# Reordering four small pieces of the attention stage: two engines copy out a low-rank sum, a scaled copy moves behind the next q and k, a weight conversion moves behind the masks, one load moves behind another

## The chip, the cores and the metric

One core of one Trainium2 chip runs the whole kernel. The metric is device microseconds of one execution; the median of three runs of the kernel before is 671.45 us (670.75 to 672.5).

## The reference

A block-wise linear attention with a decay per head is followed by a channel mixer whose token mixing is a low-rank product. In short:

```python
# attention: B=4 batches, H=8 heads, S=768 positions, D=64
for each block of positions:
    intra = (q @ k.T * decay_mask) @ v
    inter = (q * lam**(pos+1)) @ kv_state
    out   = intra + inter
    kv_state = lam**block * kv_state + (k * lam**rev).T @ v
x = out, heads side by side          # (4, 768, 512)
# mixer: U (768, 32), V (32, 768), w_ch1 (512, 2048), w_ch2 (2048, 512), some of them in 8-byte floats
u   = x + (x.T @ U @ V).T
out = u + relu(u @ w_ch1) @ w_ch2
```

## The kernel before

**Tiles and steps.** The 4 x 768 positions are cut into 24 tiles of 128 positions, six to a batch. The attention stage is one loop over the tiles, s = 0 to 23, and c = s modulo 6 is the place in the batch. The order of every instruction in this stage is written out by hand: the list `pieces` (L629 to L657) holds names of small functions, and the loop at L761 calls them one after the other. Each engine runs its own share of that list strictly in this order, so a piece that stands earlier in the list can hold up everything behind it on the same engine.

**One step.** In step s the pieces do the following, in this order. `prep(s+1)` (L368) transposes the next tile's q and k on PE into the PSUM tile `pqk`, and ACT copies them out as `qt` and `kt` (L364). From the eighth step on, `turn` (L571) transposes a finished tile of u (L600) and `mix` (L544) adds the low-rank product (L551), both into `pm`. `scale` and `fade` let POOL and ACT multiply q, k and the state by the decay (L390, L379, L399). `split` and `mixed` are DVE's part of `turn` and `mix` (L620, L621, L563). `intra(s)` multiplies the masked scores `sm` with v into the PSUM tile `px` (L444), `state(s)` makes the next state in a PSUM tile that shares its place with `pqk` (L424), and `inter(s)` adds the old state's part to `px` (L455); then ACT copies `px` out as `x_nat` (L461). `turned` (L606 to L610) is the last part of `turn`: ACT writes the high part of u (L607) and POOL the difference (L608). `scores(s+1)` makes the next scores on PE (L406), and `masked(s+1)` multiplies them with the decay mask on DVE into `sm` (L415), for which the next step's `intra` waits. There is one buffer each for `px`, `pqk`, `pm` and the scores `pss`, so each is free again only when its reader is through.

**Batch ends.** In the last step of batches 0 to 2 (s = 5, 11, 17) `low` (L466) makes x^T U: 24 matmuls (48 in the records, two passes each) into 32-row groups of a PSUM tile `pp` that takes the place of `px`, and ACT copies the four groups to one row block `p_f` (L481). `low_rows` (L483) splits it: DVE makes the high part `p_h` (L511), and in the next step `next_of_low` lets ACT copy `p_h` to four places (L519), POOL make the low part (L523), and ACT copy that on (L530).

**Conversions beside it.** U, V and the weights come as 8-byte floats and are turned into floats by steps of their own, which `aside(s)` (L724) runs at given s. V's conversion is at s = 0, 3, 4 and 5. At s = 4 it has three DVE instructions (L186, L191, L689), and the same call issues a load of 128 KB of w_ch1's words. V's high part (four ACT copies, L696) is held back by `on_scalar_late` to step 5.

**Loads.** SP issues all loads but the first of k, in order. Before the loop it issues the first three tiles of q, k and v, with U's words (192 KB, `aside(-1)`) ahead of the third q. Later tiles are issued by `load_next` inside `prep` and `state`. There are three buffers for q and for v, and four for k.

**After the attention stage** come the first product of the mixer (L806, L816), into whose first units the last batch's low-rank work is threaded, and the second product (L939 to L943). Both are long rows of matmuls of 128x512.

Of the kernel before, what the change touches and what calls it, by code (L numbers as in the profile page):

```python
# [14 lines left out]
P = 128  # L15
# [3 lines left out]
def kernel(  # L19
# [28 lines left out]
    nc = tc.nc  # L48
# [3 lines left out]
    NT = S // P  # L52
# [4 lines left out]
    R = moe_U.shape[1]  # L57
    G = P // R
# [39 lines left out]
    def tmp(name):  # L98
        return wconv.tile([P, C], FP32, tag="tmp", bufs=3, name=name)
# [97 lines left out]
    def split_steps(tile_of, src, in_parts=False, scale=None, apart=False):  # L197
# [16 lines left out]
        def six():  # L214
            w, low = st["w"], st["o"][:, 1, :]
            st["low"] = low.bitcast(FP32) if scale is None else w
            nc.vector.tensor_tensor(
                out=low if scale is None else w, in0=w, in1=st["t"], op=ALU.subtract
            )
            if scale is not None:  # L220
                on_scalar(lambda: nc.scalar.mul(low, w, scale))
# [30 lines left out]
    def two_banks(name, tag):  # L252
        return psf.tile([P, 2, N], FP32, tag=tag, name=name)
# [7 lines left out]
    def bank(shape, name, tag):  # L261
        return psa[0].tile(shape, FP32, tag=tag, bufs=2, name=name)
# [8 lines left out]
    def load(name, s, engine):  # L271
        b, c = divmod(s, NT)
        t = raw_pool.tile(
            [P, H, D], FP32, tag=f"{name}raw", bufs=4 if name == "k" else 3, name=f"{name}raw"
        )
        source = {"q": q, "k": k, "v": v}[name]
        n = H if name == "v" else H // parts(s)
        for h in range(0, H, n):
            engine.dma_start(
                out=t[:, h : h + n, :],  # L280
                in_=source[b, h : h + n, c * P : (c + 1) * P, :].rearrange("h p d -> p h d"),
            )
        raw[s, name] = t
# [52 lines left out]
    kv = {}  # L336
# [124 lines left out]
        nc.scalar.copy(xs[s].rearrange("p (a x e) -> p x a e", a=HP, x=2), px)  # L461
        del st[s]

    pps = {}

    def low(b):  # L466

        pp = two_banks("pp", "px")[:, 0, 0:P] if b < B - 1 else bank([P, P], "pp", "b2")
        for c in range(NT):
            for g in range(G):  # L470
                nc.tensor.matmul(  # L471
                    out=pp[g * R : (g + 1) * R, :], lhsT=u_w[:, c, :],
                    rhs=xs[b * NT + c][:, g * P : (g + 1) * P],
                    start=(c == 0), stop=(c == NT - 1),
                )
        if b == B - 1:
            pps[b] = pp
            return
        pps[b] = rows_f = tmp("p_f")[0:R]
        for g in range(G):  # L480
            nc.scalar.copy(rows_f[:, g * P : (g + 1) * P], pp[g * R : (g + 1) * R])  # L481

    def low_rows(b):  # L483

        pp, t = pps.pop(b), tmp("p_h")[0:R]
        own = [(slice(g * R, (g + 1) * R), slice(g * P, (g + 1) * P)) for g in range(G)]
        if b == B - 1:
            h, h2, l, l2 = (p_hl[g * R : (g + 1) * R] for g in range(G))
            for rows, cols in own:
                nc.vector.tensor_scalar(  # L490
                    t[:, cols].bitcast(U32), pp[rows].bitcast(U32), HI, None, ALU.bitwise_and
                )

            def low_part():
                for rows, cols in own:
                    nc.vector.tensor_tensor(
                        out=l[:, cols], in0=pp[rows], in1=t[:, cols], op=ALU.subtract
                    )

            def spread():  # L500
                nc.scalar.copy(h, t)
                nc.scalar.copy(h2, t)

            def spread_low():
                nc.scalar.copy(l2, l.bitcast(FP32))

            pps[b] = [spread, low_part, spread_low]
            return

        rows_f = pp  # L510
        nc.vector.tensor_scalar(t.bitcast(U32), rows_f.bitcast(U32), HI, None, ALU.bitwise_and)  # L511
        wide = [slice(x * 2 * P, (x + 1) * 2 * P) for x in range(2)]

        def place(g, low):
            return p_hl[g * R : (g + 1) * R, wide[low]]

        def spread():
            for g in range(G):
                nc.scalar.copy(place(g, 0), t[:, wide[g // 2]])  # L519

        def low_part():
            for x in range(2):
                nc.gpsimd.tensor_tensor(  # L523
                    out=place(2 * x, 1), in0=rows_f[:, wide[x]], in1=t[:, wide[x]],
                    op=ALU.subtract,
                )

        def spread_low():
            for x in range(2):
                nc.scalar.copy(place(2 * x + 1, 1), place(2 * x, 1).bitcast(FP32))  # L530

        pps[b] = [spread, low_part, spread_low]
# [32 lines left out]
    uhl, ud, turned = {}, {}, {}  # L565
# [5 lines left out]
    def turn(s):  # L571

        g, n = divmod(s, TG)
        if n == 0:
            uhl[g] = hl_at[g >= FG].tile([P, 2, CT, N], F32R, tag="hl", name="u_hl")
            ud[g] = d_at[g >= FG].tile([P, CT, N], F32R, tag="d", name="u_d")
        cols = slice(n * P, (n + 1) * P)
        hi, low, diff = uhl[g][:, 0, :, cols], uhl[g][:, 1, :, cols], ud[g][:, :, cols]
        if g >= FG:
            pt = bank([P, CT, P], "put", "b1")  # L580
# [49 lines left out]
    for s in range(NS):  # L630
        b, c = divmod(s, NT)
        done = s - NT - 1
        more = s + 1 < NS
        turns = done > 0 and (done - 1) // TG < FG
        mixes = 0 <= done < NS - NT - 1
        rows = c == 0 and b > 0
        step = [("prep", s + 1)] * more
        step += [("turn", done - 1)] * turns + [("mix", done)] * mixes
        step += [("mix", done + 1)] * (not more)
        step += [("next_of_low", b - 1)] * rows + [("next_of_low", b - 1)] * rows  # L640
        step += [("scale", s + 1)] * more
        step += [("fade", s)] * (c > 0)
        step += [("late", s - 1)] * (1 < s < NT - 1 or s > NT)
        step += [("split", done - 1)] * turns
        step += [("mixed", done)] * mixes + [("mixed", done + 1)] * (not more)
        step += [("next_of_low", b - 1)] * rows
        step += [("intra", s), ("state", s), ("inter", s)]
        step += [("late", s)] * (s < 2 or s in (NT - 1, NT))
        step += [("turned", done - 1)] * (done > 0)
        step += [("scores", s + 1)] * more  # L650
        step += [("low", b)] * (more and c == NT - 1)
        step += [("aside", s)] * (0 < s < NT - 1 or s > NT)
        step += [("masked", s + 1)] * more
        step += [("low_rows", b)] * (more and c == NT - 1)
        step += [("aside", s)] * (s in (0, NT - 1, NT))
        step += [("store", done)] * (done >= 0 and done // TG < FG)
        pieces += step  # L657
    waiting = {name: list(range(NS)) for name in "qkv"}

    def load_next(name, engine=nc.sync):  # L660
        if waiting[name]:
            load(name, waiting[name].pop(0), engine)
# [3 lines left out]
        "prep": prep, "fade": fade, "scores": scores, "masked": masked, "inter": inter,  # L666
        "intra": intra, "state": state,
        "low": low, "low_rows": low_rows, "next_of_low": next_of_low, "mix": mix, "turn": turn,
        "mixed": mixed, "store": store, "split": lambda s: splits.pop(s)(),
        "scale": scale, "turned": lambda s: turned.pop(s)(),  # L670
# [53 lines left out]
    def aside(s):  # L724
        late.insert(0, None)
        for step in side.pop(s, ()):
            step()
        late.pop(0)
# [15 lines left out]
    load_next("k", nc.scalar)  # L744
    for name in "qkvkv":
        load_next(name)
    aside(-1)
    for name in "qkv":
        load_next(name)
    make_identity(nc, ident)  # L750
    pl = two_banks("pl", "pss")[:, 0, 0:H]
# [108 lines left out]
    c0, b = NS - NT, B - 1  # L860
# [131 lines left out]
    for i in range(len(steps) - STAG):  # L992
        g, ft = steps[i]
# [49 lines left out]
```

## Time and profile before

| What | Value |
|---|---|
| median of three runs | 671.45 us |
| the profiled execution | 669.36 us, of it 667.5 us span |
| PE busy | 656.7 us (98% of the span) |
| DVE / ACT / POOL busy | 490.1 / 281.5 / 115.1 us |
| chain that ended last | PE 94%, ACT 3%, DMA 2%, issue 1% |
| attention stage | 0 to about 117 us of the span |
| DMA share from 0 to 100 us | 0.84 to 1.03 in each stretch of 10 us |

The span is what the engines' records cover; the execution's own time lies 1.9 us above it. Times such as "at 64.6" are microseconds from the start of the span. In a row of the timeline the first two figures are start and length, and the bracket at the end is idle time of that engine just before the row with what ended it. In the chain of waits each piece is start, length and who held the chain.

### The profile page before, as it was taken

The numbers are of one execution on the slowest core, as the hardware profiler recorded it, in microseconds if no ns is written. First come the engines' busy times: TensorE is split into PE (matmuls) and PEld (weight loads), VectorE is DVE, ScalarE is ACT, GpSimd is POOL, SyncE is SP. The second block draws the span as 40 slices with busy tenths as digits, with TensorE's granted clock in tenths as the row PEclk, the third lists the DMA queues.
The fourth block names the chain that finished last, engine by engine and source line by source line (L and its number), as shares of the span: only waits on it lengthen the run. The fifth ranks groups of instructions, "written<-read, shape, count | busy, mean of one in ns | idle before, by whom it ended". The sixth has DMA issues, their size and how long they took to land.

```text
span 667.5 us, 13397 instructions
## 1 busy us (share of the span) xinstructions
PE 656.7 (98%) x5242; PEld 539.0 (81%) x5242; DVE 490.1 (73%) x856; ACT 281.5 (42%) x536; POOL 115.1 (17%) x98
## 2 busy tenths in 40 slices
PE   8899999999999999999999999999999999999997
PEld 7789889788888888888888888888888888888885
DVE  5669989878999777777796255886676775865864
ACT  4677886554555444444453122332322322322320
POOL 4456877330000000000000000030030300300300
PEclk9999999999999999999999999999999999999999
DMA  8999994354776655555578999753263352543531
GB/s 193 224 224 239 229 251 133 127 190 161 273 249 240 213 203 201 200 202 202 199 265 296 319 310 396 273 194 121 92 215 97 124 190 94 170 145 96 164 89 63
DMA packets 131776, 131.29 MB, mean 197 GB/s; under 512 B 81346, under 2 KB 89794, under 8 KB 131714
## 3 DMA queue, kind: packets, MB, share of 16 engines
q1 hardware_dynamic: 130512, 130.05, 61.3%
q8 instruction: 41, 0.67, 0.4%
q10 hardware_dynamic: 1202, 0.39, 0.2%
q14 instruction: 21, 0.17, 0.1%
HBM read 80.09 MB, written 50.33 MB: 195 GB/s over the span
## 4 chain that ended last, share of the span: by engine, by line
PE 94%; ACT 3%; DMA 2%; issue 1%; DVE 0%; ACTq 0%; DVEq 0%
PE pz L806 27%; PE pz L941 13%; PE pd L816 13%; PE pz L939 13%; PE pd L943 13%; PE pss L406 3%; PE px L444 3%; PE px L455 2%; PE pkv L424 1%; PE pqk L358 1%; DMA qraw<-in_q_dram 1%; DMA vraw<-in_v_dram 1%; PE pp L471 1%; DMA kraw<-in_k_dram 1%; PE pm L551 1%
## 5 line engine op out<-in xcount | busy, mean ns | idle before, releaser
L806 PE MATMUL pz<-u_hl,w 128*128 128x512 f32 x768 | 190.0, 397 | 0.0
L806 PEld LDWEIGHTS pz<-u_hl,w 128*128 128x128 f32 x768 | 144.0, 188 | 35.2 <-ACT r L812 0.3
L941 PE MATMUL pz<-w_hl,m 128*128 128x512 f32 x384 | 151.1, 396 | 0.0
L939 PE MATMUL pz<-w_hl,m 128*128 128x512 f32 x384 | 150.9, 396 | 0.0
L943 PE MATMUL pd<-w_d,m 128*128 128x512 f32 x384 | 149.5, 396 | 0.0
L922 ACT ACTIVATE m<-mt 128x512 fp32r<-128x512 f32 x96 | 60.6, 632 | 196.3 <-PE pd L943 134.0
L923 DVE SCALAR_TENSOR_TENSOR m<-rm,m 128x512 fp32r<-128x512 f32 x96 | 71.4, 745 | 51.4 <-ACT m L922 51.2
L968 POOL TENSOR_TENSOR o<-o,u 128x512 f32<-128x512 f32 x20 | 29.8, 1523 | 447.4 <-DVE o L964 447.4
L821 DVE SCALAR_TENSOR_TENSOR r<-pd,r 128x512 f32<-128x512 f32 x96 | 61.8, 685 | 53.9 <-ACT r L812 43.5
L816 PE MATMUL pd<-u_d,w 128*128 128x512 f32 x384 | 98.6, 397 | 0.0
L812 ACT ACTIVATE r<-pz 128x512 f32<-128x512 f32 x96 | 52.2, 596 | 93.2 <-PE pz L806 92.5
L941 PEld LDWEIGHTS pz<-w_hl,m 128*128 128x128 f32 x384 | 72.3, 188 | 17.7
L939 PEld LDWEIGHTS pz<-w_hl,m 128*128 128x128 f32 x384 | 72.3, 188 | 17.6
L943 PEld LDWEIGHTS pd<-w_d,m 128*128 128x128 f32 x384 | 72.3, 188 | 17.6
L816 PEld LDWEIGHTS pd<-u_d,w 128*128 128x128 f32 x384 | 72.1, 188 | 17.3
L924 DVE SCALAR_TENSOR_TENSOR m<-m 128x512 fp32r<-128x512 f32 x96 | 69.0, 721 | 0.9
L921 DVE TENSOR_SCALAR mt<-rm 128x512 uint32<-128x512 uint32 x96 | 46.1, 481 | 28.5 <-DMA rm<-r_d 27.9
L415 DVE TENSOR_TENSOR sm<-pss,mask 128x512 f32<-128x512 f32 x48 | 30.9, 684 | 8.8 <-PE pss L406 8.5
L212 ACT CAST w<-wt 128x512 fp32r<-128x512 f32 x32 | 19.9, 621 | 30.5 <-DVE wt L209 23.4
L444 PE MATMUL px<-vraw,sm 128*64 128x64 f32 x768 | 28.3, 226 | 3.7 <-ACT kt L364 1.8
L444 PEld LDWEIGHTS px<-vraw,sm 128*64 128x64 f32 x768 | 25.1, 137 | 7.3 <-ACT kt L364 1.9
L406 PE MATMUL pss<-qt,kt 64*128 64x128 f32 x384 | 28.8, 291 | 0.0
(95 smaller groups left out, 667.1 us busy)
## 6 DMA issues: line engine op xcount, KB each, us to landing
r_d<-r SPq DMA_DIRECT2D x96, 256.0 KB, 2.5
rm<-r_d SPq DMA_DIRECT2D x96, 256.0 KB, 2.7
words<-in_moe_w_ch_dram SPq DMA_DIRECT2D x30, 512.0 KB, 4.3
w_d<-w SPq DMA_DIRECT2D x16, 768.0 KB, 3.3
w_hl<-w_d SPq DMA_DIRECT2D x16, 512.0 KB, 6.6
vraw<-in_v_dram SPq DMA_DIRECT2D x24, 256.0 KB, 5.0
u_d<-x_nat SPq DMA_DIRECT2D x24, 256.0 KB, 3.9
u<-u_d SPq DMA_DIRECT2D x24, 256.0 KB, 4.1
```

The costliest lines, as they stand in the source:

```text
L406: nc.tensor.matmul(out=pss[:, x, a, :], lhsT=kt[half[x], a, :], rhs=qt[half[x], a, :], start=True, stop=True,)
L444: nc.tensor.matmul(out=px[half[t], x, a, :], lhsT=sm[:, x, a, half[t]], rhs=vr[:, 2 * a + x, :], start=(a == 0), stop=(alone and a == HP - 1),
L806: nc.tensor.matmul(out=acc[g][0], lhsT=w[:, n, ct, :], rhs=uhl[g][:, n, ct, :], start=(ct == 0 and n == 0), stop=(ct == CT - 1 and n == 1),)
L812: nc.scalar.mul(rs[g], acc[g][0], 4096.0 + 1.0)
L816: nc.tensor.matmul(out=acc[g][1], lhsT=w[:, 2, ct, :], rhs=ud[g][:, ct, :], start=(ct == 0), stop=(ct == CT - 1),)
L821: nc.vector.scalar_tensor_tensor(rs[g], acc[g][1], 4096.0, rs[g], ALU.mult, ALU.add)
L922: nc.scalar.activation(out=m[:, 0], in_=t, func=AF.Relu)
L923: nc.vector.scalar_tensor_tensor(m[:, 1], r, 0.0, hi, ALU.max, ALU.subtract)
L924: nc.vector.scalar_tensor_tensor(m[:, 2], hi, E, low, ALU.mult, ALU.subtract)
L939: nc.tensor.matmul(out=pz, lhsT=m[:, 0, cols], rhs=hl[:, 0], start=first, stop=False)
L941: nc.tensor.matmul(out=pz, lhsT=m[:, 1, cols], rhs=hl[:, 1], start=False, stop=end)
L943: nc.tensor.matmul(out=pd, lhsT=m[:, 2, cols], rhs=dd, start=first, stop=end)
```

## The change

Four edits, all in the attention stage:

1. `low` now has ACT copy only the first two of the four groups of `pp`. The other two are copied by DVE in `low_rows`, that is behind `masked(s+1)`. This is for batches 0 to 2.
2. `turned` for the tile that is turned in a batch's first step (s = 12 and 18) no longer runs at the end of that step, but in the next one (s = 13 and 19), behind `prep`, `scale` and `fade` and ahead of `split`. It is one ACT and one POOL instruction each time.
3. `aside(4)`, with V's three DVE instructions and the load of w_ch1's words, moves from before `masked(5)` to behind it.
4. The third tile of q is issued ahead of U's words.

```diff
@@ low
         pps[b] = rows_f = tmp("p_f")[0:R]
-        for g in range(G):
+        for g in range(2):
             nc.scalar.copy(rows_f[:, g * P : (g + 1) * P], pp[g * R : (g + 1) * R])
+        others[b] = pp
@@ low_rows
-        rows_f = pp
+        rows_f, pp = pp, others.pop(b)
+        for g in range(2, G):
+            nc.vector.tensor_copy(
+                out=rows_f[:, g * P : (g + 1) * P], in_=pp[g * R : (g + 1) * R]
+            )
         nc.vector.tensor_scalar(t.bitcast(U32), rows_f.bitcast(U32), HI, None, ALU.bitwise_and)
@@ pieces
         step += [("late", s - 1)] * (1 < s < NT - 1 or s > NT)
+        step += [("turned", done - 2)] * (done > 1 and c == 1)
         step += [("split", done - 1)] * turns
...
         step += [("late", s)] * (s < 2 or s in (NT - 1, NT))
-        step += [("turned", done - 1)] * (done > 0)
+        step += [("turned", done - 1)] * (done > 0 and c > 0)
         step += [("scores", s + 1)] * more
         step += [("low", b)] * (more and c == NT - 1)
-        step += [("aside", s)] * (0 < s < NT - 1 or s > NT)
+        step += [("aside", s)] * (0 < s < NT - 2 or s > NT)
         step += [("masked", s + 1)] * more
         step += [("low_rows", b)] * (more and c == NT - 1)
-        step += [("aside", s)] * (s in (0, NT - 1, NT))
+        step += [("aside", s)] * (s in (0, NT - 2, NT - 1, NT))
@@ loads ahead of the loop
     for name in "qkvkv":
         load_next(name)
+    load_next("q")
     aside(-1)
-    for name in "qkv":
+    for name in "kv":
         load_next(name)
```

More of the change, by code (lines that the diff above doesn't have):

```diff
@@ L462, in inter @@
         del st[s]
-    pps = {}
+    pps, others = {}, {}
     def low(b):
```

## The prediction

> **What bounds the kernel now.** I read the page first, then the chain of waits in order of time, then the timeline where the chain leaves PE.
>
> ```profile
> PE 656.7 (98%) x5242; PEld 539.0 (81%) x5242; DVE 490.1 (73%) x856; ACT 281.5 (42%) x536; POOL 115.1 (17%) x98
> PE 94%; ACT 3%; DMA 2%; issue 1%; DVE 0%; ACTq 0%; DVEq 0%
> ```
>
> PE is the bound nearly everywhere; the change adds and removes no PE work. What it can win lies in the 6% (about 40 us) of the chain that is not PE, and the chain from 117 us on is PE without a break. So only the attention stage counts, and there only the places where PE stands. The chain shows four kinds. First, loads: the third to fifth steps wait for q and v (rows one and two below). Second, step 4 to step 5, the rest of this fence:
>
> ```profile
> 17.22 0.46 PE L358 MATMUL pqk<-ident,qraw 64*128 64x64 f32 x8 [0.30 <-DMA qraw<-in_q_dram]
> 26.89 1.15 PE L444 MATMUL px<-vraw,sm 128*64 128x64 f32 x32 [0.54 <-DMA vraw<-in_v_dram]
> ...
> 29.07 1.16 PE L406 MATMUL pss<-qt,kt 64*128 64x128 f32 x16
> 29.66 1.17 DVE L186 SCALAR_TENSOR_TENSOR sc<-words,sc 64x384 uint32<-64x384 uint32 x1 [0.62 <-ACT sc L168]
> 30.87 0.55 DVE L191 SCALAR_TENSOR_TENSOR vf<-m,sc 64x384 f32<-64x384 f32 x1
> 31.45 0.35 DVE L689 TENSOR_SCALAR vt<-vf 64x384 uint32<-64x384 uint32 x1
> 31.73 1.27 DVE L415 TENSOR_TENSOR sm<-pss,mask 128x512 f32<-128x512 f32 x2
> 32.50 1.24 PE L444 MATMUL px<-vraw,sm 128*64 128x64 f32 x32 [1.78 <-ACT kt L364]
> ```
>
> The bracket names ACT's `kt`, but these matmuls read `sm` and v. The scores were ready near 30.3 and DVE was in V's conversion until 31.8; `sm` starts at 31.73 and PE 0.77 us later, when the first half of `sm` (0.64) is done. DVE is the true cause. Third and fourth, the batch ends (chain of waits, batch 1):
>
> ```profile
> 64.61 0.26 ACT p_f L481
> ...
> 65.70 0.47 ACT qt L364
> 66.18 0.59 ACT kt L364
> ...
> 69.20 0.58 ACT x_nat L461
> 69.78 0.02 issue
> 69.81 0.04 ACT u_hl L607
> 69.85 0.50 issue
> 70.34 0.57 ACT qt L364
> 70.91 0.50 ACT kt L364
> 71.41 0.04 issue
> 71.45 0.69 PE pkv L424 x16
> ```
>
> From 64.61 to 71.41 the chain is ACT without a gap: four `p_f` copies, q and k, six copies of the rows, `x_nat`, u's high part, q and k again. PE's `pkv` waits at the end because it takes the place of `pqk`, which `kt` frees. Batch 2 is the same from 92.10 to 98.90; at batch 0 four V copies (L696) stand ahead of `p_f`.
>
> **What the skill says.** (1) "VectorE: DVE Perf Modes", section "The TRN2 errata — SBUF-src ops pay a fixed extra latency per instruction", prices a PSUM copy of 128 elements at (120+128)/0.96 = 258 ns on VectorE and (172+128)/1.2 = 250 ns on ScalarE. The trace agrees: ACT's `p_f` copies are 258 ns; DVE's nearest row, L490 on the same shape from `pp`, is 283. (2) "PSUM — Partial Sum Buffer", section "PSUM bank collisions raise a hardware error": two engines may read one bank at once if they keep to different groups of 32 partitions. The two halves do so, and the kernel before never tries it. But in the changed program's order of instructions the first DVE copy waits for ACT, while `p_h`, which reads all four groups, waits for DVE alone. So that wait must cover ACT's copies: the halves run one after the other. (3) "SBUF — State Buffer", section "Who interferes with whom": a VectorE operation with two SBUF inputs and a GpSimd operation that reads SBUF block each other. L186 agrees: 1.17 us beside POOL's `ks` (28.34 to 30.42), where the same shape in L178 took 0.55.
>
> **The change, part by part** (s is the step; all times from the one profiled execution).
>
> *V's conversion behind the masks.* Three DVE instructions (1.17+0.55+0.35) leave the way of `masked(5)`. In steps without a delay `sm` starts 1.21 after `pss` (10.99 to 12.20, 44.60 to 45.81). So `sm` starts at 29.07+1.21 = 30.28 and `px` at 31.05 instead of 32.50: **1.45 us**. PE is ready (transposes end at 30.72), v of step 5 landed at 29.9. The three now run from 31.6 and end by 33.7 even at their old lengths; `sm(6)` starts at 35.50-1.45 = 34.05, and the V copies on ACT start at 33.5, behind `x_nat`. So they stay covered; uncovered they would cost up to 0.2. The words' load in the same call keeps its place, as masks issue no DMA.
>
> *Two of four `p_f` copies to DVE.* ACT loses 2 x 0.27 = 0.53 us at each batch end. DVE's two start when ACT's end: 0.53 + 0.05 + 2 x 0.283 = 1.15 against 1.07 before, so `px` comes free, and `p_h` starts, about 0.1 later. DVE has nothing to do there in between (idle 1.3 ahead of `p_h`); queued behind are the next tile's split, which waits for PE until 65.4 anyway, and `pkv`'s copy at 67.96. PE waits for this DVE copy before the next `px`: from 65.73 to 65.83 at batch 1. Batch 0 is different: its `px` is late by ACT's V copies, and what follows is all ACT, so the 0.53 shows in full at `x_nat(6)`: 41.74-1.45-0.53 = 39.76, and `px(7)` at 40.40 instead of 42.38. PE's own way there (36.75 for `px(6)`, then 3.65) gives 40.40 too. Up to here **1.98 us**.
>
> *u's high part behind the next q and k.* One ACT copy (0.63, pitch 0.50) and one POOL instruction (1.28) at s = 12 and 18. Batch 1: `kt` ends at 71.41-0.53-0.50 = 70.38. PE now comes last: `px(12)` 65.83, plus 3.89 (the time from 65.73 to 69.62, where its `pm` was through) is 69.72 for `px(13)`, and `pkv` 0.98 later at 70.70. From there a regular step of 4.30 (74.82 to 79.12) leads to `px(14)` at 74.02 instead of 74.82: **0.80 us**, and from 93.22 to 102.31 in batch 2 the same sum gives **0.80**. What is moved lands between `fade` (ends 71.2) and `x_nat(13)` (71.9), a hole of 0.7 for 0.63. If it doesn't fit, `x_nat` has over 1 us before PE asks. On POOL `qs` and `ks` now go ahead of it, which only helps.
>
> *Third q ahead of U's words.* One load of 256 KB passes one of 192 KB on SP. That q lands some 0.7 earlier than 12.40 and lets `px(1)` start 0.2 sooner, but the fourth q lands at 17.09 behind the same bytes and PE waits for it at 17.22. Likewise v at 26.76. U's words land by 12.4; DVE takes them at 15.74. I take **0**, with bounds of a gain of 0.2 (PE was otherwise ready at 26.70) and a loss of 0.3.
>
> **Sum:** 1.98+0.80+0.80 = 3.58. The profiled execution would go from 669.36 to 665.8, the span from 667.5 to 663.9. The runs' median lies 2.1 above that execution; on it the sum gives 671.45-3.6 = **667.9**.
>
> Unknown: the DVE copy and its handover. Below, halves that do run side by side free `px` 0.5 sooner, but PE then limits: 0.23 more at each of the last two batch ends and nothing at the first, 667.4. Above, 0.42 a copy (L430, a PSUM copy twice as long): 0.28 later at all three, 668.7. I take 0.283, as the shape and the source are the same.
>
> **Rivals.**
> - *The loads are the true pace.* From v of step 7 (37.71) to v of step 20 (97.58) landings take 59.87 us, their uses 59.93, and the DMA share from 40 to 100 is 0.89 to 1.03. For it: the equality. Against: PE waits for no load after 27 us, and v lands 2.8 to 5 us ahead. If landings don't move at all, v of step 17 (85.04) allows 87.83-85.17 = 2.66 there, then 0.80: 668.0, hardly different. If a pause of the queue falls badly and half the gain goes, 669.7.
> - *The gain is given back in the first product*, or only V's part works: 671.45-1.45 = 670.0. Against: the chain from 117 to 146 is PE alone.
> - *Slower: the start's pauses move onto the loads that PE waits for.* SP stands twice in an issue, 2.74 us from 12.53 and 2.85 from 22.09. Both now fall behind the q and v that set 17.22 and 26.89. If the new order puts both ahead, these two, with no slack, are late by 5.6: 667.9+5.6 = 673.5. It decides once v of step 4 lands 3.6 later than 26.76. Against: bytes and number of loads ahead of both are the same.
> - *It doesn't do what it says:* the DVE copies do wait for ACT, so the two engines don't share the time. That is in my sum; by itself it would leave 0.1 a batch end lost.
>
> **How the numbers follow.** Forecast, 667.4 to 668.7: 0.66. Part of the gain lost (about 669.7, some of it beyond 0.3%): 0.16. Only V's part: 0.10. Slower: 0.08. A measurement of this kernel can tell about 0.3%, or 2.0 us, from no change, so faster means below 669.4: 0.66+0.11 = 0.77; same 0.15; slower 0.08. The range goes from 666.0 (667.4 less 0.2 of the start and about 1 us by which medians of this kernel vary) to 670.0 (only V's part), with about 2 in 10 outside.
>
> **What would show it.** In the profile after: `sm` of step 5 starting 1.21 behind its `pss`, with V's three DVE rows after it; ACT's chain at the batch ends two copies shorter; `pkv` two steps later waiting for PE, not `kt`; DVE's copies starting after ACT's second; the first product starting near 113.6 instead of 117.15. I am wrong if that start is later than 115.7, if PE waits for loads after step 4, or if DVE's copies take over 0.4 us.

## The result, and the profile after

The changed kernel takes 667.34 us (median of 20 runs, 665.44 to 670.22) against 670.62 us for the kernel before (20 runs): ratio 0.9952, 95% interval 0.9939 to 0.9965, so 3.3 us less where 3.6 were forecast. The profiled execution took 666.27 us against 669.36, its span 664.5 against 667.5.

The page after, the busy times and the shares of the chain that ended last:

```profile
PE 655.4 (99%) x5242; PEld 539.2 (81%) x5242; DVE 491.6 (74%) x862; ACT 280.2 (42%) x530; POOL 115.7 (17%) x98
PE 96%; DVE 1%; ACT 1%; DMA 1%; issue 0%; ACTq 0%; DVEq 0%
```

Six instructions went from ACT to DVE (530 for 536, 862 for 856). ACT's share of the chain fell from 3% to 1%, and DVE, which had none, has 1%: this is the first sign of who ends last at a batch end now. From the first product on, the two traces run at the same pace: in the chain of waits it starts at 114.08 instead of 117.15 (3.07 less), and the span ends 3.06 earlier. All of the gain was made in the attention stage and none was given back.

Where it was made, from the starts of `px` (L444) in the two timelines:

| Stretch | before | after | difference |
|---|---|---|---|
| start to step 4 | 26.89 | 26.61 | -0.28 |
| step 4 to 5 (V's conversion) | 5.61 | 4.25 | -1.36 |
| 5 to 7 (batch end 0) | 9.88 | 9.42 | -0.46 |
| 7 to 11 | 17.70 | 17.92 | +0.22 |
| 11 to 14 (batch end 1) | 14.74 | 14.03 | -0.71 |
| 14 to 17 | 12.90 | 13.32 | +0.42 |
| 17 to 20 (batch end 2) | 14.59 | 13.90 | -0.69 |
| 20 to the first product | 14.77 | 14.56 | -0.21 |

The 0.22 of steps 7 to 11 is no effect of the edits: step 7 to 8 takes 4.68 us in this trace and 4.34 to 4.39 in five of the experiments' traces (`e1`, `e6`, `e7`, `e11`, `e12`), since PE pauses within its `pkv` group (1.01 us instead of 0.73; see "Pauses of PE" at the end).

Each sum of the prediction can be held against one row. V's conversion, in the timeline after:

```profile
28.86 1.16 PE L406 MATMUL pss<-qt,kt 64*128 64x128 f32 x16
30.07 1.29 DVE L415 TENSOR_TENSOR sm<-pss,mask 128x512 f32<-128x512 f32 x2 [1.22 <-PE pss L406]
30.86 1.24 PE L444 MATMUL px<-vraw,sm 128*64 128x64 f32 x32 [0.35 <-issue]
31.28 0.54 DVE L186 SCALAR_TENSOR_TENSOR sc<-words,sc 64x384 uint32<-64x384 uint32 x1
31.85 0.55 DVE L191 SCALAR_TENSOR_TENSOR vf<-m,sc 64x384 f32<-64x384 f32 x1
32.44 0.35 DVE L695 TENSOR_SCALAR vt<-vf 64x384 uint32<-64x384 uint32 x1
```

`sm` starts 1.21 behind `pss` and waits for PE; V's three rows stand behind it. L186 takes 0.54 instead of 1.17, as POOL's `ks` beside which it ran has ended (28.25 to 30.33).

Batch end 1, in the chain of waits after (start, length, holder):

```profile
63.28 0.28 DVE p_f L513
...
63.58 0.30 DVE p_f L513
...
63.90 0.42 DVE p_h L516
...
64.35 0.70 DVE ut L625
...
65.07 0.69 DVE u_hl L626
65.77 0.60 DVE x_nat L568
66.36 0.34 DVE kv L430
...
66.75 0.71 PE pqk L358 x16
```

In the kernel before this stretch was ACT from end to end. Now it is DVE's queue without a gap: the two new copies, `p_h`, the split, the addition, and last the copy of the state, which frees the place of `pqk` for PE's next transposes. After that PE holds the chain. The wait for `kt` ahead of `pkv` is gone: in the timeline `kt` runs to 68.63 and `pkv` starts at 68.91 with no bracket.

```profile
68.04 0.59 ACT L364 COPY kt<-pqk 128x512 f32<-128x512 f32 x1
68.91 0.64 PE L424 MATMUL pkv<-vraw,ks 128*64 128x64 f32 x16
70.66 2.70 POOL L613 TENSOR_TENSOR u_d<-u_hl 128x512 fp32r<-128x512 f32 x2
...
74.55 1.06 POOL L379 TENSOR_TENSOR ks<-kraw,small 128x512 f32<-128x512 f32 x1
74.77 1.39 DVE L217 TENSOR_TENSOR w<-wf,wt 128x512 fp32r<-128x512 f32 x1
76.08 1.28 DVE L415 TENSOR_TENSOR sm<-pss,mask 128x512 f32<-128x512 f32 x2
```

The last four rows hold the new loss: POOL runs the moved `u_d` and the next one in a single stretch, and is busy from there through `qs`, `ks` and the next `u_d` (to 77.29). DVE's weight step L217, with the mask of step 15 behind it, now begins 0.22 behind POOL's `ks` and takes 1.39. In the kernel before it began 0.69 behind it and took 0.93:

```profile
76.67 1.07 POOL L379 TENSOR_TENSOR ks<-kraw,small 128x512 f32<-128x512 f32 x1
...
77.36 0.93 DVE L217 TENSOR_TENSOR w<-wf,wt 128x512 fp32r<-128x512 f32 x1
```

In both traces L217 ends 0.55 us behind POOL's instruction: 0.84 of `ks` were left when it began now, 0.38 before. Step 14 to 15 takes 4.63 us instead of 4.30.

### The profile page after: what moved, and what is told of

Same layout as the page of the kernel before. It is cut to its first block, busy times and chain, and to the rows that moved or that the text cites. A ratio compares the mean times of both kernels' runs of the same rounds, so it can differ in the third digit from the quotient of the medians.

```text
span 664.5 us, 13398 instructions
## 1 busy us (share of the span) xinstructions
PE 655.4 (99%) x5242; PEld 539.2 (81%) x5242; DVE 491.6 (74%) x862; ACT 280.2 (42%) x530; POOL 115.7 (17%) x98
## 4 chain that ended last, share of the span: by engine, by line
PE 96%; DVE 1%; ACT 1%; DMA 1%; issue 0%; ACTq 0%; DVEq 0%
PE pz L813 27%; PE pz L948 14%; PE pz L946 14%; PE pd L823 14%; PE pd L950 13%; PE px L444 4%; PE pss L406 4%; PE px L455 2%; PE pqk L358 2%; PE pkv L424 1%; PE pp L471 1%; DMA kraw<-in_k_dram 1%; PE pm L556 1%; PE put L587 1%; PE pm L605 0%
## 5 line engine op out<-in xcount | busy, mean ns | idle before, releaser
L444 PE MATMUL px<-vraw,sm 128*64 128x64 f32 x768 | 29.1, 229 | 3.5 <-issue 1.4
L444 PEld LDWEIGHTS px<-vraw,sm 128*64 128x64 f32 x768 | 26.1, 141 | 6.9 <-issue 2.6
(96 smaller groups left out, 667.5 us busy)
```

Of the source, the lines that this page charges most:

```text
L444: nc.tensor.matmul(out=px[half[t], x, a, :], lhsT=sm[:, x, a, half[t]], rhs=vr[:, 2 * a + x, :], start=(a == 0), stop=(alone and a == HP - 1),
```

## The experiments

**Each edit alone, on the kernel before.** Theory: the parts add up as forecast. Rival: they overlap, or one of them carries all. The first edit is that of V's conversion:

```diff
-        step += [("aside", s)] * (0 < s < NT - 1 or s > NT)
+        step += [("aside", s)] * (0 < s < NT - 2 or s > NT)
...
-        step += [("aside", s)] * (s in (0, NT - 1, NT))
+        step += [("aside", s)] * (s in (0, NT - 2, NT - 1, NT))
```

> Only V's conversion moves behind the masks. Theory (DVE's conversion held the masks of step 5): the first matmul of step 5 comes 1.4 us sooner against that of step 4 (4.2 instead of 5.6 us behind it), all later steps keep the gain, the first product starts 1.45 us sooner; time down by 1.45 us. Rival (ACT's four V copies at the batch end take it back): step 5 sooner by 1.4, but steps 7 and later not; time unchanged.

Measured: 669.62 us, ratio 0.9976 (0.9963 to 0.9989). Step 4 to 5 takes 4.26 us instead of 5.61, which is 1.35 less (the next three kernels, which keep V's conversion in its place, take 5.75 to 5.80 there). The stretches behind it are those of the kernel before within 0.1 us; the gain is kept, so the rival is out. The start to step 4 took 28.91 in this trace, because PE paused for 1.65 us ahead of 22.21 and was then granted half its clock from 22.84 to 26.26 (see the last section).

The second moves two `p_f` copies to DVE:

```diff
-        for g in range(G):
+        for g in range(2):
             nc.scalar.copy(rows_f[:, g * P : (g + 1) * P], pp[g * R : (g + 1) * R])
...
+        for g in range(2, G):
+            nc.vector.tensor_copy(...)
```

> Only the two groups of pp go to DVE. Theory (ACT's chain sets the batch ends, and a copy fewer on ACT shows until PE is the bound): DVE's copies start when ACT's second ends; the px behind it is 0.1 later, but two steps on the gain is 0.5 at each of the three batch ends, 1.5 to 1.6 us in all. Rival (the copies in series are what counts): 0.1 us lost at each batch end, time up by 0.3.

Measured: 669.39 us, ratio 0.9982 (0.9969 to 0.9996). Steps 11 to 14 take 14.37 us (0.37 less than in the kernel before, 0.28 less than in `e1_v_only`) and 17 to 20 take 14.23 (0.36 less). Batch end 0 can't be read: PE was granted half its clock there, from 32.95 to 36.37. What ends last at batch end 1 is still ACT's `kt`, in the timeline's row of the weight loads for `pkv`:

```profile
71.61 0.55 PEld L424 LDWEIGHTS pkv<-vraw,ks 128*64 128x64 f32 x16 [0.26 <-ACT kt L364]
```

The third moves `turned`:

```diff
+        step += [("turned", done - 2)] * (done > 1 and c == 1)
         step += [("split", done - 1)] * turns
...
-        step += [("turned", done - 1)] * (done > 0)
+        step += [("turned", done - 1)] * (done > 0 and c > 0)
```

> Only u's high part moves behind the next q and k (steps 12 and 18). Theory: ACT reaches the k copy of two steps on 0.50 us sooner, PE's pkv waits for it no longer, gain 0.5 at each of two batch ends, 1.0 us in all. If each of this and of the copy to DVE wins 0.5 alone but both only 0.7 together, they share one wait. Rival (POOL's later difference or the tmp buffer holds the next split): nothing or a loss of up to 0.6 each.

Measured: 669.25 us, ratio 0.9977 (0.9965 to 0.9988). Steps 11 to 14 take 14.01 us (0.73 less) and 17 to 20 take 13.96 (0.63 less): alone it wins what both edits win together (0.71 and 0.69). Step 14 to 15 takes 4.63 with L217 at 1.39 us, where L217 took 0.98 in `e2_pf_only`, so the loss at L217 belongs to this edit. (Step 14 to 15 of `e2_pf_only` took 4.77 all the same: PE's `px` group of L455 took 1.16 there instead of 0.69, in a pause. Its mask started 1.21 behind `pss`, as in a step without a delay.) The last stretch, 20 to the first product, takes 14.57 as in the changed kernel, against 14.77 in `e1_v_only`, so its 0.21 is this edit's too. The fourth is the order of the loads:

```diff
+    load_next("q")
     aside(-1)
-    for name in "qkv":
+    for name in "kv":
```

> Only the third q ahead of U's words. Prediction's step (the loads behind have the same bytes ahead of them): no change at the first matmuls of steps 2 and 4, time unchanged. Rival, suggested by the changed kernel, whose v of step 4 landed at 26.05 instead of 26.76: v of step 4 lands some 0.7 us sooner, step 4 starts 0.3 sooner, time down by 0.3 us, which only the trace can tell.

Measured: 670.0 us, ratio 0.9989 (0.9975 to 1.0002). Step 4 starts at 25.83 us, against 25.92 and 26.02 in `e2_pf_only` and `e3_turned_only`, which keep the old order, and v of step 4 landed between 25.59 and 25.79 us in all four kernels of this group. So no effect can be told from zero.

**Taking one edit out of the whole.** The edits of `p_f` and `turned` meet at one wait, so the question is what `p_f` adds beside the other. `e6_without_pf` is the changed kernel with all four copies on ACT.

> The changed kernel with all four p_f copies on ACT again, as in the kernel before (V's conversion, turned and the third q stay moved). Theory (p_f and turned lift the same wait at batch ends 1 and 2, so that p_f adds nothing there on top): steps 11 to 14 and 17 to 20 take the 14.0 and 13.95 us of the changed kernel, only batch end 0 (steps 5 to 7) goes back from 9.42 to 9.87; time 0.45 above the changed kernel's, ratio to the kernel before 0.9958. Rival (the gains add: p_f is worth 0.36 at each batch end, as alone): 14.37 and 14.3 there, time 1.2 above, ratio 0.997.

Measured: 667.54 us, ratio 0.9959 (0.9943 to 0.9974). Steps 5 to 7 take 9.86 us instead of 9.42, and steps 11 to 14 take 14.09 instead of 14.03. Steps 17 to 20 took 14.87 in this trace, but step 17 alone took 6.42 where all other kernels' with aligned loads take 5.50 to 5.63: PE stood still in the middle of a group for reasons that the profile doesn't show.

```profile
87.15 0.68 PE L455 MATMUL px<-kv,qs 64*64 64x64 f32 x28
...
88.44 0.33 PE L455 MATMUL px<-kv,qs 64*64 64x64 f32 x4 [0.61 <-issue]
```

So `p_f` is worth 0.44 at batch end 0 and about 0.06 at batch end 1, where alone it was worth 0.37: the rival, that the gains add, is out. For batch end 2 that trace can't say it as sharply.

**Do DVE's copies wait because they share `p_f` with ACT's?** `e5_own_rows` gives them a buffer of their own, which the tile `lam_row` of the start is laid into.

```diff
-        pps[b] = rows_f = tmp("p_f")[0:R]
+        pps[b] = rows_f = tmp("p_f")[0:R, 0 : 2 * P]
...
+        rows_g = p_g
         for g in range(2, G):
             nc.vector.tensor_copy(
-                out=rows_f[:, g * P : (g + 1) * P], in_=pp[g * R : (g + 1) * R]
+                out=rows_g[:, (g - 2) * P : (g - 1) * P], in_=pp[g * R : (g + 1) * R]
             )
-        nc.vector.tensor_scalar(t.bitcast(U32), rows_f.bitcast(U32), HI, None, ALU.bitwise_and)
...
+        for x, part in ((1, rows_g), (0, rows_f)):
+            nc.vector.tensor_scalar(
+                t[:, wide[x]].bitcast(U32), part.bitcast(U32), HI, None, ALU.bitwise_and
+            )
...
-    lam_row = consts.tile([1, H + P], FP32, name="lam_row")
+    p_g = consts.tile([R, 2 * P], FP32, name="p_g")
+    lam_row = p_g[0:1, 0 : H + P]
```

POOL's low part reads `rows_f` and `rows_g` in turn.

> The changed kernel, but DVE's two groups go to row buffer p_g of their own, so that nothing in them waits for ACT's two copies; DVE makes p_h in two halves (32x256 each), and POOL's low part reads the two buffers. Theory (DVE's pair ran in series because it shared p_f with ACT's pair): DVE's copies start with ACT's, near 62.75 instead of 63.28 at batch end 1; px(12) then starts when PE ends pm, at about 63.78 instead of 63.97, and DVE's queue behind it (p_h, ut, u_hl, x_nat, kv) is about 0.45 earlier, so that PE's next transposes need not wait for kv (0.26 at 66.75). Some 0.2 to 0.3 at batch ends 1 and 2, and about 0.6 at batch end 0, where PE stood 0.70 before px(6): 1.1 in all, ratio to the kernel before 0.9935. Rival A (the handover is not what they wait for: PSUM read by two engines, or DVE's queue behind the masks): DVE's copies start at the same place or take 0.5 us each, gain 0, ratio 0.995. Rival B (at batch end 0 something else is late, x_nat of ACT): 0.5 in all, ratio 0.9945.

Measured: 671.23 us, ratio 1.0013 (1.0000 to 1.0026): about 4 us slower than the changed kernel, which none of the theories had. DVE's copies still start 0.04 after ACT's end (64.60 and 64.64 at batch end 1), so the first half of rival A holds; the 4 us were a new question. `e7_behind_10_14` and `e8_own_and_behind` ran beside it. The first moves the weight steps that stand ahead of a mask at steps 10 and 14, the second does both:

```diff
-        step += [("aside", s)] * (0 < s < NT - 2 or s > NT)
+        step += [("aside", s)] * (0 < s < NT - 2 or (s > NT and s not in (10, 14)))
...
-        step += [("aside", s)] * (s in (0, NT - 2, NT - 1, NT))
+        step += [("aside", s)] * (s in (0, NT - 2, NT - 1, NT, 10, 14))
```

> The changed kernel, with the weight steps of steps 10 and 14 behind the masks as well, as V's are at step 5; DVE has L186 at step 10 and L217 at step 14 behind the two masks instead of ahead of them. Theory (the 0.33 given back between step 14 and 15 is L217 at 1.39 us ahead of sm(15), and the 0.28 lost between step 10 and 11 is L186 ahead of sm(11)): both intervals are 4.30 instead of 4.63 and 4.58; 0.6 less, ratio 0.9943. Rival A (what is late next takes it: ut, u_hl, x_nat and the kv copy stand behind L217 and L186 on DVE, and PE's transposes of the step after wait for kv): 4.6 again, a step later, ratio 0.995. Rival B: L217 is as slow behind the masks and pushes two steps, 0.3 lost, ratio 0.9957.

Measured: 666.96 us, ratio 0.9953 (0.9935 to 0.9970). The timeline around step 15:

```profile
74.77 1.29 DVE L415 TENSOR_TENSOR sm<-pss,mask 128x512 f32<-128x512 f32 x2 [0.76 <-PE pss L406]
75.98 0.76 DVE L217 TENSOR_TENSOR w<-wf,wt 128x512 fp32r<-128x512 f32 x1
...
79.05 0.46 PE L358 MATMUL pqk<-ident,qraw 64*128 64x64 f32 x8
```

L217 now begins when 0.21 us of a POOL instruction are left and takes 0.76 instead of 1.39, again 0.55 behind that one's end (POOL's `qs`, which begins behind L217, is now the slow one, 1.75 for 1.28). Step 14 to 15 takes 4.30 instead of 4.63, step 10 to 11 4.31 instead of 4.58, as the theory has it. But step 15 to 16 takes 4.60 instead of 4.39, since DVE's copy of the state, now behind L217, ends at 78.99, right ahead of the transposes in the last row. Rival A holds for a part: of 0.60 won, 0.21 goes. In the time, the rest is below what the runs resolve.

> Both edits together on the changed kernel: the row buffer of DVE's own, and the weight steps of steps 10 and 14 behind the masks. They act at different steps, so the theory adds them: 1.1 and 0.6, 1.7 us below the changed kernel, ratio 0.9926, about 665.7. Rivals: only the one or the other holds, ratio 0.9935 to 0.9943; neither, 0.995.

Measured: 671.4 us, ratio 1.0018 (1.0007 to 1.0029): the same loss as `e5_own_rows`.

**Where the 4 us came from.** In both kernels with the new buffer the loads of the start are slow. The tile of 256 floats, where `lam_row` had 136, moves every buffer behind it by 480 bytes: in the built program the first q buffer moves from byte 121600 of each partition (475 x 256) to 122080 (476 x 256 + 224). `e9_shift_only` is the changed kernel with nothing but that shift, `e10_own_rows_aligned` is `e5_own_rows` with a shift of 512 bytes, and `e11_shift_256` the changed kernel with a shift of 256.

```diff
-    lam_row = consts.tile([1, H + P], FP32, name="lam_row")
+    lam_row = consts.tile([1, 2 * P], FP32, name="lam_row")[:, 0 : H + P]
...
# e11_shift_256: consts.tile([1, 200], ...)
# e10_own_rows_aligned: p_g = consts.tile([R, 2 * P + H], ...)[:, 0 : 2 * P]
```

> The changed kernel with nothing but the tile lam_row widened from 136 to 256 floats a row, unused: it moves every buffer behind it, the q, k and v buffers among them, by 480 bytes, as the row buffer p_g of the two kernels that came out slow did (e5_own_rows and e8_own_and_behind). Theory (their loss is no matter of DVE's copies: a load into a buffer whose place is an odd multiple of 32 bytes is slower): loads land every 1.1 to 1.2 us in the first 30 us instead of every 0.85 to 0.9, PE waits for v here and there, and the time is about 671 us, ratio to the kernel before 1.001. Rival A (the row buffer itself costs: p_h in two halves, low part from two tiles): the time of the changed kernel, ratio 0.995, loads every 0.85 to 0.9. Rival B (chance of the start, two bad kernels): the same as rival A.

Measured: 670.98 us, ratio 0.9996 (0.9981 to 1.0011). SP's issues of full tiles in the timeline, first of the changed kernel, then of this one; SP stands in each until the queue takes it:

```profile
6.29 0.85 SPq L279 DMA_DIRECT2D vraw<-in_v_dram  x1
7.18 0.85 SPq L279 DMA_DIRECT2D qraw<-in_q_dram  x1
```

```profile
6.73 1.14 SPq L279 DMA_DIRECT2D vraw<-in_v_dram  x1
7.92 1.14 SPq L279 DMA_DIRECT2D qraw<-in_q_dram  x1
```

> The row buffer of DVE's own once more, but with 8 floats more a row, so that the buffers behind it move by 512 bytes and stand on multiples of 64 again. Theory (DVE's pair waits for ACT's pair because both read the one PSUM tile pp, whatever they write to): DVE's copies start 0.03 to 0.05 after ACT's second one ends, the batch ends are those of the changed kernel, ratio 0.995 as the changed kernel's, loads every 0.85 to 0.9 us. Rival (the own buffer costs by itself): 1.001 as in e5_own_rows.

Measured: 667.04 us, ratio 0.9951 (0.9936 to 0.9966), the changed kernel's. SP's issues take 0.85 again. DVE's copies of batch end 1 start 0.04 after ACT's end (64.05), although nothing but `pp` is left that both use:

```profile
63.53 0.52 ACT L481 COPY p_f<-pp 32x128 f32<-32x128 f32 x2 [1.50 <-PE pp L471]
64.09 0.59 DVE L514 COPY p_g<-pp 32x128 f32<-32x128 f32 x2 [0.79 <-PE pqk L358]
```

The bracket names PE's transposes, which happen to end in the same moment as ACT's copy. They are not the cause: at batch end 0 of `e12_behind_and_kv_first` they ended at 35.87, when DVE, which started at 35.19, had long begun, and DVE starts 0.03 to 0.04 after ACT's second copy in every trace with this edit.

> The changed kernel with lam_row widened to 200 floats, which moves the q, k and v buffers by 256 bytes, from an odd multiple of 256 to a multiple of 512. Theory (only the multiple of 64 counts): nothing changes, ratio 0.995, loads every 0.85 to 0.9 us. Rival (the larger the power of two, the faster a load): loads every 0.75 to 0.8, the start 0.5 us earlier, ratio 0.994 or less.

Measured: 668.2 us, ratio 0.9960 (0.9945 to 0.9976), no different from the changed kernel's. The median distance of two landings in a row (loads of q, k and v issued in the first 20 us, gaps over 1.4 us left out) is 0.90 us in the changed kernel, 0.91 and 0.95 in these two, and 1.15, 1.17 and 1.16 in the three with 480 bytes. So the loss is the place of the buffers, and it is the loads that lose: the instructions of DVE, ACT and POOL in `e9_shift_only` keep the median lengths that they have in the changed kernel. How slower loads cost time differs from trace to trace. In `e9_shift_only` the first `px` stands 1.40 later (10.43 instead of 9.03) and PE has more of the pauses of the last section; in `e5_own_rows` PE also waits three times for v, 2.2 us in all. The expectations speak of multiples of 64, but the good places were all multiples of 256; which power of two counts is not told apart.

**The new bound of a batch end.** `e12_behind_and_kv_first` is `e7_behind_10_14` with DVE's copy of the state ahead of the addition in steps 12 and 18.

```diff
-        step += [("mixed", done)] * mixes + ...
+        step += [("mixed", done)] * (mixes and c > 0) + ...
...
-        step += [("intra", s), ("state", s), ("inter", s)]
+        step += [("intra", s), ("state", s)]
+        step += [("mixed", done)] * (mixes and c == 0) + [("inter", s)]
```

> The changed kernel with the weight steps of steps 10 and 14 behind the masks, and at steps 12 and 20 DVE's copy of kv ahead of its addition to x_nat instead of behind it. Theory (what ends last at batch ends 1 and 2 is now DVE's queue of p_f, p_h, ut, u_hl, x_nat and kv, for which PE's next transposes wait 0.26 us): kv is copied near 65.8 instead of 66.28, when PE has written it, the transposes start as soon as pss is done, steps 12 to 13 and 18 to 19 take 3.75 us instead of 3.96, steps 10 to 11 and 14 to 15 take 4.30 instead of 4.58 and 4.63: 0.4 and 0.4, less the 0.2 to 0.3 that step 15 to 16 may take back; ratio 0.9943. Rival A (PE is bound by itself there or ACT's kt is late next): 3.9 to 3.96 stays at steps 12 and 18, ratio 0.995. Rival B (the later x_nat holds up pm, into which PE transposes next): PE waits at pm, 0.2 to 0.4 lost at each, ratio 0.9955.

(The second of the two steps is 18, not 20 as the text has it.) Measured: 666.39 us, ratio 0.9943 (0.9922 to 0.9964). The timeline of batch end 1:

```profile
65.94 0.41 DVE L430 COPY kv<-pkv 128x256 f32<-128x256 f32 x1
66.27 0.68 DVE L568 TENSOR_TENSOR x_nat<-pm,x_nat 128x512 f32<-128x512 f32 x1
...
66.77 0.41 PE L358 MATMUL pqk<-ident,qraw 64*128 64x64 f32 x8
67.90 1.15 PE L444 MATMUL px<-vraw,sm 128*64 128x64 f32 x32
```

PE's transposes no longer wait, and steps 12 to 13 and 18 to 19 both take 3.67 us instead of 3.96 and 3.97: that DVE's queue ended last there is shown, and rivals A and B are out. This kernel has the lowest median of all, 0.95 us under the changed kernel's, but the two intervals overlap widely; that it beats it is shown in the stretches, not in the time.

## Why the prediction was right, and where its steps were off

- **V's conversion: 1.45 forecast, 1.36 measured** (1.35 alone). `sm` at `pss` + 1.21 and `px` 0.79 after that came as worked out (1.21 and 0.77 were used), L186 shortened to 0.54, and the copies stayed covered (ACT's from 33.27). Of the 0.09, 0.07 is PE's own way to `pss` (2.25 from `px(4)` instead of 2.18), the rest that handover.
- **Batch end 0: 0.53 forecast, 0.46 measured**, and 0.44 back when the edit is taken out. ACT's row of copies up to `x_nat` held the chain there, as said.
- **Batch ends 1 and 2: 0.80 each forecast, 0.71 and 0.69 measured.** The size was near, the account of it was not. The step that failed is "what comes last": I let PE come last after `px(12)`, and said of DVE that it "has nothing to do there" and that the split "waits for PE until 65.4 anyway". The chain shows the split at 64.35, straight behind `p_h`, and DVE's queue through to the copy of the state, for which PE waited until 66.75. `e12_behind_and_kv_first` freed it and won 0.29 and 0.30. That the size came out near is in part luck: the 3.89 that I took for PE's own way from `px(12)` to `px(13)` held a wait for `kt` ahead of `pkv` (1.14 from `px` to `pkv`, 0.95 in the changed kernel). PE's own way is 3.67, and DVE's queue put it back to 3.96. These 0.07 and a `px(12)` that came 0.13 later instead of 0.10 account for the 0.09 that is missing at batch end 1.
- **Which edit earns the 0.80.** The sum let the `p_f` edit and the move of `turned` both shorten the wait for `kt`. Alone they win 0.37 and 0.73, together 0.71: the move of `turned` takes nearly all of the wait away, and `p_f` adds at most 0.06 at each. Had I priced the edits one by one and added, 1.1 would have come out.
- **"`qs` and `ks` now go ahead of it, which only helps": wrong.** `turned` alone brings step 14 to 15 from 4.30 to 4.63, and moving L217 behind the masks takes that away (both shown). In four traces (before, after, `e2_pf_only`, `e7_behind_10_14`) L217 takes 0.55 us and what is left of POOL's instruction when it begins: 0.38, 0.84, 0.43 and 0.21 us. POOL's later place, not a slower DVE, makes it 1.39. The Trainium skill's "SBUF — State Buffer", section "Who interferes with whom", which I used for L186, states just this mutual blocking, and I didn't carry it to the instruction that POOL's moved work would now meet. Of the +0.42 in steps 14 to 17, 0.33 is this; `e3_turned_only` has the whole 0.42.
- **Third q: 0 forecast.** Alone 0.9989 (0.9975 to 1.0002). The 0.28 that the two traces differ by at step 4 is no gain of the edit: the kernels without it reach step 4 as early as those with it.
- **DVE's copies in series: right, with a wider reason than needed.** They took 0.28 and 0.30 (0.283 used) and started 0.03 behind ACT's. Two buffers didn't part them; what is left is the wait on the one tile `pp`, which is argued by what remains and not shown by a kernel with two such tiles. Whether two engines would get in each other's way there was not tried.
- **Rivals.** No load was waited for after step 4, so the loads' pace did not cap it, but `e9_shift_only` shows how near that is: loads slower by 0.26 us each cost 3 to 4 us. Even with aligned loads, v of step 15 landed at 78.06 in `e10_own_rows_aligned`, just ahead of its `px` at 78.20. The slower case did not come: v of step 4 landed at 26.05 instead of 26.76.
- **The sum:** 3.58 forecast for the profiled execution, 3.09 measured. The terms give 1.36+0.46+0.71+0.69 = 3.22; the start and the last steps add 0.49 (0.28 is scatter of the start, 0.21 more of the move of `turned`), and 0.64 is lost between: 0.33 at L217, 0.22 in the pause of step 7, the rest in step 15. The medians differ by 3.28, and that they come so near holds some luck: the change also takes away most executions with a stretch of half clock (last section), a term that the prediction did not have.

## What to carry to other kernels

Two edits that shorten one wait were worth little more here than the larger alone, not their sum: price each with the other in place, and ask which queue is full behind the engine that is relieved. When work is moved on POOL, list the DVE instructions that it will newly run beside. A tile added to a pool moves every buffer allocated behind it, so keep the places of load buffers where they were (here multiples of 256 bytes), and test a suspicious loss with the shift alone.

## What the runs showed of the hardware

**A load's destination.** Full tiles (2 KB in each of 128 partitions) land every 0.90 us where the buffers begin on multiples of 256 bytes and every 1.16 where they begin 224 bytes beyond one: 1.29 times as long, and 3 to 4 us on this kernel. The Trainium skill, "DMA: Bandwidth & Descriptors", section "How a descriptor splits into AXI transactions", says that a descriptor that doesn't start on 256 bytes costs extra beats. These tiles move in pieces of 256 bytes, one head of one position each (of 24051 packets of the first 30 us, 23983 lie under 512 bytes). By the page's rule, 256 bytes from byte 224 are 15 beats instead of 8, an estimate of 1.88 times, and it speaks of reads. The runs show a smaller cost, 1.29 times, for the side that is written.

**PE at half pace.** The first 32 matmuls with v (step 0), in the timeline before and then after:

```profile
9.10 1.28 PE L444 MATMUL px<-vraw,sm 128*64 128x64 f32 x32
```

```profile
9.03 1.98 PE L444 MATMUL px<-vraw,sm 128*64 128x64 f32 x32
```

The same 32 matmuls take 1.15 later on. The half pace ends near 9.1 us in the one trace and near 11.8 in the other, which put step 1 of the changed kernel 0.62 behind; by step 2 the wait for a load had covered 0.49 of it. The Trainium skill, "TensorE: Matmul & The Clock Gate", section "Part 1: The HAM clock gate", says that the switch to full pace moves from run to run by some 0.5 us. Here it moved by 2.7 between these two, and over all fourteen traces it came at 9.06 to 12.59 us. The granted clock of the windows reads 1.00 before it too, but only because the trace's clock record begins with the switch (at 9.14 and 11.84 us).

**Half clock in the middle.** Three traces hold one more stretch of granted clock 0.50, of 3.42 us each: from 22.84 in `e1_v_only`, from 32.95 in `e2_pf_only`, from 91.10 in `e8_own_and_behind`. Each came soon after PE had stood still, for 1.65, 1.89 and 1.77 us. Such a stand is not enough: ahead of step 5 PE stands 1.78 us in the kernel before and 1.88 in `e3_turned_only` and `e4_q_only`, and these traces show none. But the mean clock of most executions is on record. Where V's conversion is ahead of the masks, 80 of 209 executions have a mean of 0.997 or less, as one such stretch gives. With it behind the masks, where PE's stand of step 5 is gone, 6 of 125 have. Of the 69 executions of the kernel before that were measured beside `e1` to `e4`, those 32 have a median of 671.66 us, the others 670.01. So moving V's conversion also takes away most of these stretches, which the 1.36 us of the traces do not hold.

**Pauses of PE.** Eleven of the twelve experiments' traces hold, in the attention stage, one to four pauses of 0.2 to 1.65 us within a group of matmuls, with nothing that released them. They stood only at the 345th, 471st, 725th, 850th, 976th, 1103rd, 2116th, 2495th and 2622nd matmul record, places that lie multiples of 125 to 127 apart, and not in every run. Shorter pauses stand at these places and at others of the same spacing. The trace before has one of 0.20 at the 725th record, and the pause of step 7 in the trace after is at the 850th. The pauses are one reason why the ends of single traces scatter, and why stretches were compared. The page lists a DMA queue of kind "instruction" (q8, 41 transfers, 0.67 MB). In the traces all 21 pauses of the experiments end 1.2 to 1.85 us after the end of a transfer on this queue, while PE passes places of this spacing without a pause up to 5.3 us after one, and never less than 1.1. That fits PE waiting for instructions that come late; no run changed the fetch, so it is not shown.
